# Gates of two units in turns, decays by matrix products, other engines for the fills, and stage dates of a list schedule shifted

## The chip, the cores and the metric

The kernel runs on one core of one Trainium2 chip. A core has five engines that run side by side, each through its own list of instructions in order: TensorE (PE, matrix products), VectorE (DVE), ScalarE (ACT), GpSimd (POOL) and SyncE (SP). SP's part here is to issue DMAs; ACT and POOL issue some too. The metric is the time on the device in microseconds (us); less is better.

## What is computed

Two blocks in a row. The first is a gated linear recurrence for 4 batches, 8 heads, 768 steps and heads of 48 numbers, with complex decays whose magnitude is capped at 0.999. The second is a feed-forward block on its output, seen as 3072 tokens of 384 numbers, with a hidden size of 1536.

```python
mag = np.sqrt(a_re * a_re + a_im * a_im)
scale = np.minimum(mag, 0.999) / (mag + 1e-06)
a_re_n, a_im_n = (a_re * scale, a_im * scale)
for t in range(S):
    new_re = ar * S_re - ai * S_im
    new_im = ar * S_im + ai * S_re
    S_re, S_im = (new_re + outer(k[t], v[t]), new_im)
    y[:, :, t] = q[t] @ S_re
# x: y as (3072, 384)
xn = x / sqrt(mean(x * x) + 1e-06) * rms_g
g = xn @ w_gate
out = (g * sigmoid(g) * (xn @ w_val)) @ w_out
```

The three weight matrices arrive as 64-bit floats and are narrowed to 32 bits on the chip.

## The kernel before

**Chunks, units, groups.** The steps are cut into 24 chunks of 128 (six a batch). Units of chunks go through the gates: unit 0 is chunk 0, unit 1 is chunk 1, and from there each unit has two chunks. Groups of two chunks go through the feed-forward block.

**`gates(u)`** turns a unit's decays into running magnitudes and angles, and rotates q and k by them, so that the recurrence within a chunk becomes ordinary masked attention. Its stages by name: "size" (squares, inverse square roots, and scans that multiply up the squared magnitudes, t4), "root" (inverse square root of t4, one correction step), "turn" (arctangent, scans that add up the angles, reduction to one period, sines), "rot" (products into the tiles `rot`). ScalarE computes inverse square roots, arctangents and sines with tables that have to be loaded: roots and arctangents lie in different ones, and a sine can use the table that the arctangent left. At the end of `gates` the rotated tiles are moved by six DMAs a chunk into `kq` (96 partitions), whose transfers are kept in `moved[n]`, and six DMAs a unit move the chunk's total decays from `ends` into `decay`.

**`attend(n)`** loads v into `ve` and `vn` (six DMAs), computes masked scores into `am` (scores that the mask doesn't write stay at the zeros with which `am` is filled once), multiplies by v and by the state, updates the state by the chunk's products and decay, normalises ("norm": squares, their sum by a product with ones, a power on POOL, spreading to all partitions) and writes `xT`.

**`feed(g, xT)`** multiplies a group's `xT` by the gate and value weights in six blocks, applies the gate into `hT`, and multiplies by `wo`. Groups 0 and 1 do it plainly; from group 2 on four quadrants are combined so that seven products stand for eight, with scratch (S1, S2, T1) in the upper half of `hT`. Group 1 keeps its hidden values in that upper half (`base` 3072).

**`narrow(i)`** loads one of twelve weight pieces by a POOL DMA (three for the gate and three for the value weights, 1.5 MB each, and six for the out weights, 0.75 MB each), lets ACT convert the low words in place and DVE put the 32-bit number together in three operations. At most two pieces are under way (`AHEAD`). The first waits for unit 0's a_im (`GATE`, `begun`), and piece 3, counted from 0, waits until chunk 0's kq has landed:

```python
    CLEAR = {3: 0}
    GATE = 0
```

**What sets the order.** Nothing is issued as the functions run. Each call adds an operation to the class `Flow`, with an engine, a duration, what it reads and writes, and sometimes a date ("due"). `note` finds what an operation depends on by the bounding boxes of what it touches; two transfers whose boxes overlap are planned one after the landing of the other even where their elements don't meet. `dates` carries due dates back from the users to the makers and adds a shift by stage, which is empty before. `schedule` then plays the engines forward in a model of time and lets each take the ready operation with the earliest date, and `issue` writes the result out as the fixed order of every engine. Waits on the chip follow from the data. Arguments: `after` is a dependency, `behind` only an order of issue, `late` the earliest date. Idle stretches of PE before a set time (`WARM`) are filled with matmuls on `rot` whose results nobody reads; they keep PE's clock up.

**The main program** loads the inputs of units 0 and 1, runs `gates(0)`, then `gates(1)`, then the twelve pieces, and then chunk by chunk: the gates of the next unit, attention, and after every second chunk a feed group. After group 2 it adds checks of the weights ("look").

All operations are recorded by the same line, 667 of the kernel before, so the profile tells them apart by tile: `bank` is PSUM, `t`, `in`, `turns` are tiles of the gates, `kin` the raw q and k, and the weight pieces are staged in `wo` and `hT`.

Of the kernel before, what the change touches and what calls it, by code (L numbers as in the profile page):

```python
# [461 lines left out]
class Flow:  # L462
# [7 lines left out]
    LAND = 2.0  # L470
    LANES = 8
    turn = 0.0
    BEGIN = {"SP": 0.8, "ACT": 0.8, "POOL": 0.8}
    TABLES = {"silu": ("S",), "sin": ("S", "T"), "arctan": ("T",), "rsqrt": ("A",)}

# [28 lines left out]
    def note(self, op, ap, write):  # L504
        b = self.box(ap)
        if b is None:
            return
        name, p0, p1, lo, hi = b
        if name.startswith("bank"):
            p0, p1, lo, hi = 0, P, 0, 2048  # L510
        kept = []
        for x in self.seen.get(name, ()):
            o, w, q0, q1, l, h = x
            over = q0 < p1 and p0 < q1 and l < hi and lo < h
            if over and (write or w) and o != op["i"]:
                op["deps"].add(o)
            if not (write and p0 <= q0 and q1 <= p1 and lo <= l and h <= hi):
                kept.append(x)
        kept.append((op["i"], write, p0, p1, lo, hi))
        self.seen[name] = kept  # L520

    def add(self, eng, calls, dur, reads=(), writes=(), table=None, land=None, due=None, after=(), behind=(), late=None, mode=None):
        op = dict(i=len(self.ops), eng=eng, calls=calls, dur=dur, deps=set(), table=table, land=land,
                  base=due, late=late, mode=mode, stage=self.stage, behind={o["i"] for o in behind})
        self.ops.append(op)
        op["deps"].update(o["i"] for o in after)
        for ap in reads:
            self.note(op, ap, False)
        for ap in writes:
            self.note(op, ap, True)  # L530
        return op
# [23 lines left out]
    def schedule(self):  # L555
# [33 lines left out]
        while True:  # L589
            best = None  # L590
            for eng, ops in waiting.items():
                if ops:
                    t = max(free[eng], min(ready[o["i"]] for o in ops))
                    if eng == "SP" and len(sent) >= self.LANES:
                        if "landed" not in sent[-self.LANES]:
                            continue
                        t = max(t, sent[-self.LANES]["landed"])
                    if best is None or t < best[0]:
                        best = (t, eng)
            busy = [q for q in lanes.values() if q]  # L600
            if busy:
                whole = sum(q[0][1]["packet"] for q in busy)
                q = min(busy, key=lambda q: q[0][0] / q[0][1]["packet"])
                t = now + max(0.0, q[0][0]) * whole / q[0][1]["packet"]
                if best is None or t <= best[0]:
                    flows(t)
                    now = max(now, t)
                    o = q.pop(0)[1]
                    o["landed"] = now + o["slow"] + self.LAND + (1.5 if o["eng"] == "POOL" else 0.0)
                    release(o, o["landed"])  # L610
                    continue
            if best is None:
                break
            t, eng = best
            pick = None
            for o in waiting[eng]:
                if ready[o["i"]] > t + 1e-9:
                    continue
                key = o["due"]
                if o["table"] and table not in self.TABLES[o["table"]]:  # L620
                    key += self.switch
                if eng == "PE" and o["mode"] != mode:
                    key += self.turn
                if pick is None or key < pick[0]:
                    pick = (key, o)
            o = pick[1]
            waiting[eng].remove(o)
            dur = o["dur"]
            if o["table"] and table not in self.TABLES[o["table"]]:
                table = self.TABLES[o["table"]][-1]  # L630
                dur += 1.3
                self.loads = getattr(self, "loads", 0) + 1
            if eng == "PE" and o["mode"] != mode:
                mode = o["mode"]
                dur += 0.06
            if eng == "PE" and self.warm and t < self.warm["until"]:
                since = max([free["PE"]] + [x["end"] + self.SYNC for x in self.warm["after"] if not recent])
                n = int((t - since - 0.3) / 0.43)
                if n > 0:
                    self.fillers.append((order - 0.5, n))  # L640
                    recent.append((since, since + 0.43 * n))
            if eng == "PE":
                busy = sum(min(e, t) - max(b, t - 4.0) for b, e in recent if e > t - 4.0)
                if busy < 2.0:
                    dur += min(dur, 3.0)
                recent.append((t, t + dur))
                del recent[:-12]
            o["start"], o["end"], o["order"] = t, t + dur, order
            order += 1
            free[eng] = t + dur  # L650
            release(o, t + dur, self.next)
            if o["land"] is not None:
                flows(t)
                now = max(now, t)
                if eng != "POOL":
                    sent.append(o)
                lanes.setdefault(eng, []).append([o["load"] + 0.05, o])
            else:
                release(o, t + dur)
# [10 lines left out]
def fast(tc, ctx, qT, kT, v, a_re, a_im, w_gate, w_val, w_out, rms_g, out, H, bad):  # L670
# [194 lines left out]
    for t, x in ((ones, 1.0), (halfpi, PI / 2), (mid, -(RE_MAX + RE_MIN) / 2),  # L865
                 (width, -(RE_MAX - RE_MIN) / 2), (mhalf, -0.5), (zeros, 0.0)):
        fill(t, x)
    LATE = 12.0
    for t in ves + states:
        fill(t[:, :, :, D:], 0.0, late=LATE)  # L870
    add("POOL", [(make_identity, (nc, ident), {})], 0.6, [], [ident], late=LATE)
    fill(causal, 1.0, late=LATE)
    for e in range(2):
        for b in range(4):
            x = causal[b * BLK:(b + 1) * BLK, e]
            add("POOL", [(nc.gpsimd.affine_select, (), dict(out=x, in_=x, pattern=[[1, C]],
                                                            compare_op=ALU.is_ge, fill=0.0,
                                                            base=-BLK * (3 - b if e else b),
                                                            channel_multiplier=-1))], 0.3, [x], [x], late=LATE)
    for t in ams:  # L880
        fill(t, 0.0, late=LATE)
    for t in banks[4:6]:
        fill(t, 0.0, eng="DVE")
    dma(gcol, rms_g.rearrange("(c p) -> p c", p=P))


# [15 lines left out]
    AHEAD = 2  # L902
    landed = {}

    CLEAR = {3: 0}

    def fetch(i, piece, raw, eng):
        to, ap, c, f = piece
# [60 lines left out]
    moved = {}  # L969
    HOLD = 1  # L970
    begun = []
    started = []
    cleared = {}
    loaded = {}
# [6 lines left out]
    def load_gates(u):  # L981
# [14 lines left out]
        t["kq"], t["k"], t["q"] = x, x[:, :, 0], x[:, :, 1]  # L996
        for name, ap in (("re", a_re), ("im", a_im)):
            x = dma(t[name], ap[b].rearrange("(h j l) s -> l h j s", j=ND, l=L)[:, :, :, c * C:c * C + T],
                    "ACT" if u < 2 and name == "im" else "SP", behind=moved[HOLD] if u > 1 else ())
            if u < 2 and x["eng"] == "SP":  # L1000
                rows_.append(x)
        if u == GATE:
# [3 lines left out]
    def load_kq(u, t):  # L1006
        flow.stage = "kq", u
        for name, ap in (("q", qT), ("k", kT)):
            for i, n in enumerate(UNITS[u]):
                dma(t[name][:, :, i * C:(i + 1) * C],  # L1010
                    ap[n].rearrange("d (h t) -> (d h) t", t=C).rearrange("(j p) t -> p j t", p=P),
                    behind=moved[HOLD] if u > 1 else rows_)
        return t

    def gates(u):
        ns = UNITS[u]
# [43 lines left out]
        stt(t2, t1, 1.5, t2, ALU.add)  # L1060
        tt(q, q, t4)

        flow.stage = "turn", u
        act(im, im, AF.Arctan, after=[root])
        last = turn.get(u - 1) if ns[0] % NCH else None
        for j in range(ND):
            scan(t3[:, j], im[:, j], zeros[:, 0:T], last[:, j] if last is not None else 0.0,
# [21 lines left out]
        for n_ in ns:  # L1089
            moved[n_] = [dma(kqs[n_ % 2][r:D2:2 * ND], rots[n_ % 2][:, r], "SP") for r in range(2 * ND)]  # L1090
            if n_ < 2:
                cleared[n_] = copy(seen, kqs[n_ % 2][:, 0, 0:1], eng="POOL")
        for r in range(2 * ND):
            dma(decays[way_of(u)][r:D2:2 * ND], ends[:, r % ND, ns[0]:ns[0] + nt], behind=moved[ns[0]])

# [7 lines left out]
    def attend(n):  # L1105
# [1 line left out]
        ve, am, kq = ves[n % 3], ams[n % 2], kqs[n % 2]  # L1107
        first, last = n % NCH == 0, n % NCH == NCH - 1
        vv = vns[0]
        later = dict(behind=moved[min(n - 1, HOLD)] if n else ())  # L1110
        rows = v[n * C:(n + 1) * C, :].rearrange("t (m e d) -> t m e d", e=2, d=D)
        dma(ve[:, :, 0, 0:D], rows[:, :, 0], **later)
        for b in range(4):
# [118 lines left out]
    def feed(g, xT):  # L1232
        flow.stage = "feed", g
        ns = GROUPS[g]
        T = len(ns) * C
        base = {1: 3072}.get(g, 0)
        h = hT[:, base:base + NF * T].rearrange("p (i f t) -> p i f t", i=2, f=NF)
        A = {(i, k): h[:, i, k * HD:(k + 1) * HD] for i in range(2) for k in range(2)}
        S3, S4 = A[1, 0], S2
# [65 lines left out]
        loaded[u] = load_gates(u)  # L1305
    for u in range(2):
        load_kq(u, loaded[u])
    gates(0)
    gates(1)
    for i in range(len(pieces)):  # L1310
        narrow(i)
    gated = 2
    for n in range(N):
        while gated < NU and UNITS[gated][0] <= n:
            gates(gated)
            gated += 1
        xT = attend(n)
        if n == GROUPS[group_of[n]][-1]:
# [13 lines left out]
    for in_, limit, op in ((ef, P_MIN, ALU.is_ge), (ef, 1.0, ALU.is_le), (range_, 0.0, ALU.is_le),  # L1332
# [14 lines left out]
    filler = rots[0][:, 0]  # L1347
    flow.warm = dict(after=started, until=WARM, call=[
        (nc.tensor.matmul, (banks[3][:, 0:C],), dict(lhsT=filler[:, 0:C], rhs=filler[:, C:2 * C], start=True, stop=True))])
    flow.schedule()  # L1350
    with tc.manual_schedule():
        flow.issue()
# [50 lines left out]
```

## Time and profile before

| what | us |
|---|---|
| time, median of three runs | 730.87 (729.05 to 731.51) |
| time of the profiled execution | 727.01 |
| its span, first to last instruction | 725.3 |
| PE busy | 682.6 (94%) |
| DVE busy | 470.0 (65%) |
| ACT busy | 332.3 (46%), 86.0 of it 67 table loads |
| POOL busy | 70.4 (10%) |
| first matmul with a gate weight | 57.33 |

The page divides the span into 40 slices of 18 us and gives each engine a digit of tenths for each; PEclk is PE's granted clock in tenths of full speed. The chain of waits follows the work that ended last back to what released it, with start and length of each piece. A name such as "kq<-rot" reads: written tile from read tile. SPq is SP's queue of DMA issues, and the time given for a DMA instruction there is its issue and not its transfer.

### The profile page before, as it was taken

Reading aid. Unit: us, or ns where it says so; the run is one execution under the profiler, and the core shown is the slowest. Engines: PE = TensorE matmul, PEld = TensorE weight load, DVE = VectorE, ACT = ScalarE, POOL = GpSimd, SP = SyncE. Lnnn points to the kernel's source line nnn. Section 1 sums busy time; section 2 is a strip of 40 time slices with the busy share of each in tenths; the row PEclk is TensorE's granted clock in tenths of the full one; section 3 lists DMA queues with packets and bytes.
Section 4 is the critical chain, followed back from the end, with each engine's and each line's share of the span. In section 5 each row is a group of like instructions: output and inputs, shape, how many; then the busy total and the mean of one; then the engine's idle time right before and its main releaser. Section 6 shows DMA issues by size and latency. Waiting matters only on the chain.

```text
span 725.3 us, 16217 instructions
## 1 busy us (share of the span) xinstructions
PE 682.6 (94%) x6870; PEld 596.2 (82%) x6870; DVE 470.0 (65%) x740; ACT 332.3 (46%) x450; POOL 70.4 (10%) x116
## 2 busy tenths in 40 slices
PE   0579999999999999999999999999999999999996
PEld 0468867886889889889889889889889889889885
DVE  5969898888879878879774656658544333134121
ACT  7639858867385864845461633626310110010010
POOL 6123100001100001011011011011011011000000
PEclk9978999999999999999999999999999999999998
DMA  8696665655466464566533333334133132100000
GB/s 296 214 310 190 194 185 156 180 143 128 132 149 155 142 168 119 164 141 170 140 87 76 85 63 63 100 67 91 42 62 61 37 66 34 36 13 2 23 0 27
DMA packets 105728, 81.84 MB, mean 113 GB/s; under 512 B 43664, under 2 KB 96144, under 8 KB 105648
## 3 DMA queue, kind: packets, MB, share of 16 engines
q1 hardware_dynamic: 100432, 64.99, 32.9%
q0 software_dynamic: 4416, 15.35, 9.2%
q8 instruction: 56, 0.92, 0.5%
q10 hardware_dynamic: 800, 0.39, 0.2%
q14 instruction: 24, 0.20, 0.1%
HBM read 55.84 MB, written 4.72 MB: 83 GB/s over the span
## 4 chain that ended last, share of the span: by engine, by line
PE 83%; DVE 5%; DMA 4%; ACT 3%; SPq 2%; issue 1%; POOL 0%; DVEq 0%; ACTq 0%
PE bank L667 83%; DMA ve<-in_v_dram 2%; SPq L667 2%; ACT turns L667 1%; DVE rot L667 1%; DVE turns L667 1%; DMA wo<-in_w_gate_dram 1%; ACT t L667 1%; ACT L667 1%; DMA kq<-rot 1%; DVE hT L667 1%; DMA in<-in_a_re_dram 1%; DVE in L667 0%; DVE t L667 0%; DVE wo L667 0%
## 5 line engine op out<-in xcount | busy, mean ns | idle before, releaser
L667 PE MATMUL bank<-xT,wg 128*128 128x256 f32 x864 | 200.9, 383 | 0.9 <-DVE xT L667 0.9
L667 PE MATMUL bank<-xT,wv 128*128 128x256 f32 x864 | 201.2, 382 | 0.4 <-DVE xT L667 0.4
L667 PEld LDWEIGHTS bank<-xT,wg 128*128 128x128 f32 x864 | 162.2, 191 | 22.8 <-DVE xT L667 1.1
L667 PEld LDWEIGHTS bank<-xT,wv 128*128 128x128 f32 x864 | 161.3, 190 | 23.5 <-issue 1.6
L667 ACT ACTIVATE sg<-bank 128x512 f32<-128x512 f32 x72 | 43.0, 597 | 169.4 <-PE bank L667 168.8
L667 PE MATMUL bank<-wo,hT 128*128 128x192 f32 (+1 forms) x576 | 117.7, 356 | 0.6 <-DVE hT L667 0.6
L667 DVE TENSOR_TENSOR hT<-bank,sg 128x512 f32<-128x512 f32 x72 | 49.5, 688 | 100.1 <-PE bank L667 88.5
L667 PEld LDWEIGHTS bank<-wo,hT 128*128 128x128 f32 x576 | 95.7, 190 | 12.9 <-DVE hT L667 1.1
L667 ACT ACT_TABLE_LOAD x67 | 86.0, 1283 | 16.1 <-DVE rot L667 7.1
L667 POOL TENSOR_TENSOR rs<-ssv,mhalf 128x1 f32<-128x1 f32 x24 | 25.3, 1054 | 498.6 <-DVE ssv L667 468.2
L667 DVE TENSOR_TENSOR rot<-kin,turns 128x768 f32<-128x768 f32 x48 | 44.1, 952 | 3.8 <-DMA kq<-rot 3.4
L667 PE MATMUL bank<-sums,hT 128*128 128x192 f32 x240 | 44.2, 327 | 0.0
L667 ACT ACTIVATE kt<-bank 128x384 f32<-128x384 f32 x40 | 19.2, 486 | 51.9 <-PE bank L667 32.3
L667 ACT ACTIVATE turns<-in 128x768 f32<-128x768 f32 (+1 forms) x39 | 30.1, 791 | 26.5 <-DVE rot L667 14.2
L667 PE MATMUL bank<-am,ve 128*32 128x128 f32 x768 | 39.2, 281 | 0.9 <-DMA ve<-in_v_dram 0.9
L667 PEld LDWEIGHTS bank<-sums,hT 128*128 128x128 f32 x240 | 39.7, 190 | 0.1
L667 PEld LDWEIGHTS bank<-kq 96*32 96x32 f32 x1536 | 30.2, 110 | 10.9 <-issue 7.0
L667 DVE TENSOR_TENSOR hT<-hT 128x768 f32<-128x768 f32 x40 | 38.2, 956 | 0.6
L667 PE MATMUL bank<-kq 96*32 96x128 f32 (+3 forms) x1536 | 35.2, 235 | 3.0 <-DMA kq<-rot 2.9
L667 PE MATMUL bank<-rot 128*128 128x128 f32 x64 | 12.2, 352 | 24.8 <-DVE rot L667 24.8
L667 DVE COPY_PREDICATED am<-causal,bank 128x512 f32<-128x512 int32 x48 | 33.9, 724 | 1.6 <-PE bank L667 1.1
L667 ACT ACTIVATE t<-t 128x768 f32<-128x768 f32 (+1 forms) x39 | 30.9, 792 | 8.7 <-DVE t L667 8.2
(115 smaller groups left out, 741.9 us busy)
## 6 DMA issues: line engine op xcount, KB each, us to landing
kq<-rot SPq DMA_DIRECT2D x144, 128.0 KB, 3.0
kin<-in_q_dram SPq DMA_DIRECT2D x24, 192.0 KB, 3.3
kin<-in_k_dram SPq DMA_DIRECT2D x24, 192.0 KB, 3.4
wo<-in_w_gate_dram SPq DMA_DIRECT2D x6, 768.0 KB, 5.0
out_dram<-ot SPq DMA_DIRECT2D x24, 192.0 KB, 2.2
wo<-in_w_val_dram SPq DMA_DIRECT2D x6, 768.0 KB, 5.7
wo<-in_w_out_dram SPq DMA_DIRECT2D x6, 768.0 KB, 4.3
in<-in_a_re_dram SPq DMA_DIRECT2D x11, 384.0 KB, 6.1
```

Source lines behind the costliest of these rows:

```text
L667: fn(*args, **kw)
```

## The change

It has six parts.

1. `gates` becomes a generator that stops after "root". Units 0 and 1 are run in turns: both up to the roots, then both from the turns on. The arctangent now depends on the last two units' roots.
2. `send_decays` is new. For units 0 and 1 the decays reach `decay` by a product with a selection matrix `pick` and a copy from PSUM, not by six DMAs each. The matrices for it (`pick`, `band`, `head`) are made once at the start in tiles that are free then. Later units send by DMA as before.
3. The fills: `am` 0 and the pads of `ve` and the states go from POOL to DVE, `am` 1 to a ScalarE copy of zeros, `ident` is made first, and the causal mask is cut by five selections and not eight.
4. `CLEAR` lets weight piece 3 wait for chunk 1's kq and not chunk 0's, and group 1's `hT` base is 0.
5. The planner: operations of one `group` (a chunk's v transfers, a unit's q and k transfers) don't depend on each other; ACT and DVE may be left idle in the plan for up to 1.5 us when a far more urgent operation is about to become ready; the fillers' start is counted only once their source is planned; the first loads get early dates.
6. A table of some 90 shifts of due dates by stage and number.

```diff
@@ Flow.note, Flow.add
-            if over and (write or w) and o != op["i"]:
+            if over and (write or w) and o != op["i"] and (not op["group"] or self.ops[o]["group"] != op["group"]):
                 op["deps"].add(o)
...
@@ Flow.schedule
+            if eng in self.patient:
+                for x in waiting[eng]:
+                    if t < ready[x["i"]] < t + o["dur"] - 0.2 and x["due"] < o["due"] - 50.0 and ready[x["i"]] < t + 1.5:
+                        pick = None
+                        free[eng] = max(free[eng], min(ready[y["i"]] for y in waiting[eng] if t < ready[y["i"]]))
+                        break
+                if pick is None:
+                    continue
...
@@ fast, at the start
+    add("POOL", [(make_identity, (nc, ident), {})], 0.5, [], [ident], due=-150.0)
...
+    fill(ams[0], 0.0, eng="DVE", due=-290.0)
+    act(ams[1], zeros[:, 0:C].unsqueeze(1).to_broadcast([P, H, C]), AF.Copy, due=-290.0)
     for t in ves + states:
-        fill(t[:, :, :, D:], 0.0, late=LATE)
...
-    for t in ams:
-        fill(t, 0.0, late=LATE)
...
+        fill(t[:, :, :, D:], 0.0, eng="DVE", due=-280.0)
+    pick = ots[0][:, 0:ND * D2].rearrange("p (r x) -> p r x", r=ND)
+    band, head = (ots[1][:, o:o + n] for o, n in ((0, P // H), (16, H)))
+    own = [ots[1][:, o:o + ND * H].rearrange("p (r h) -> p r h", r=ND) for o in (32, 64)]
+    fill(pick, 0.0, eng="DVE", late=LATE)
+    for o, order in ((band, "p (x h) -> p x h"), (head, "p (x h) -> p h x")):
+        add("DVE", [(nc.vector.tensor_reduce, (), dict(out=o, in_=ident.rearrange(order, h=H), axis=mybir.AxisListType.X,
+                                                       op=ALU.add))], 0.3, [ident], [o], late=LATE)
+    for r in range(ND):
+        o = pick[:, r].rearrange("p (x j) -> p x j", j=2 * ND)[:, :, r::ND]
+        copy(o, band.unsqueeze(2).to_broadcast([P, P // H, 2]), late=LATE)
...
-    CLEAR = {3: 0}
+    CLEAR = {3: 1}
...
+    def send_decays(u):
+        ns = UNITS[u]
+        if u < 2:
+            tt(own[u], ends[:, :, u:u + 1].to_broadcast([P, ND, H]), head.unsqueeze(1).to_broadcast([P, ND, H]))
+            ps = banks[u][0:D2, 0:H]
+            mms([(ps, pick[:, r], own[u][:, r], r == 0, r == ND - 1) for r in range(ND)], 0.5)
+            copy(decays[u][:, :, 0], ps)
+            return
+        for r in range(2 * ND):
+            dma(decays[way_of(u)][r:D2:2 * ND], ends[:, r % ND, ns[0]:ns[0] + len(ns)], behind=moved[max(ns[0], 1)])
...
@@ gates
+        roots.append(root)
+        yield
         flow.stage = "turn", u
-        act(im, im, AF.Arctan, after=[root])
+        act(im, im, AF.Arctan, after=roots[-2:])
...
@@ feed
-        base = {1: 3072}.get(g, 0)
+        base = 0
...
@@ main program
-    gates(0)
-    gates(1)
+    firsts = [gates(0), gates(1)]
+    for x in firsts * 2:
+        next(x, None)
...
-            gates(gated)
+            list(gates(gated))
...
+    flow.shift = {
+        ("attend", 1): 2.2, ("attend", 2): -6.5, ("attend", 4): -25.0, ("attend", 6): -11.5, ("attend", 8): 2.6,
...
+        ("w", 0): -2.4, ("w", 1): 1.0, ("w", 2): 0.3, ("w", 5): -13.7, ("w", 6): 5.7, ("w", 8): -5.6,
+        ("w", 10): 7.1, ("w", 11): 6.2,
+    }
```

## The prediction

> **What bounds the kernel now.** I read the page from the top, then the chain of waits in order of time, then the issues of SP's queue, then the busy time by stage. The page first:
>
> ```profile
> span 725.3 us, 16217 instructions
> ...
> PE   0579999999999999999999999999999999999996
> ...
> PEclk9978999999999999999999999999999999999998
> ```
>
> TensorE (PE) is full from the fourth slice on; only the first 60 us have room, and there the granted clock falls too. So a gain has to come from the start, and the view to ask is what the first feed group (its first matmul is at 57.33) waited for. The chain of waits, in order of time (start, length, what):
>
> ```profile
> 24.79 0.55 SPq L667
> ...
> 30.54 8.23 DMA ve<-in_v_dram
> 38.78 0.59 SPq L667
> ...
> 40.28 6.54 DMA ve<-in_v_dram
> ...
> 46.96 4.48 PE bank L667 x64
> ...
> 53.79 1.21 POOL rs L667
> ...
> 55.04 26.66 PE bank L667 x118
> ```
>
> The attention of chunk 1 (matmuls at 46.96) waited for its v rows (ve), which went out late and landed slowly. SP's issues say why they were late:
>
> ```profile
> 22.46 4.16 SPq L667 DMA_DIRECT2D kq<-rot  x6
> 26.66 3.84 SPq L667 DMA_DIRECT2D decay<-ends  x6
> 30.54 0.60 SPq L667 DMA_DIRECT2D ve<-in_v_dram  x1
> 33.67 3.79 SPq L667 DMA_DIRECT2D kq<-rot  x6
> 37.73 3.16 SPq L667 DMA_DIRECT2D ve<-in_v_dram  x4
> ```
>
> Chunk 0's q and k, six decays, one v transfer, then a wait until unit 1's rotated q and k are ready (33.67), then the rest of v. Last, the busy time by stage (columns: PE, PE's weight loads, VectorE (DVE), ScalarE (ACT), POOL, clock, DMA share, GB/s):
>
> ```profile
> 0.00:57.33 57.33, 25.30 (x368) 22.50 (x369) 44.05 (x62) 35.34 (x58) 20.08 (x46) 0.90 0.85 266
> 57.33:101.20 43.87, 43.16 (x393) 35.95 (x392) 41.33 (x56) 34.51 (x44) 6.29 (x12) 0.98 0.68 206
> ```
>
> Of the 25.30 us of PE before 57.33, 12.2 are fillers (bank<-rot, x64). After 57.33 PE runs to 718.84 with about 4.2 us of idle (by windows: 0.7 to 101.2, 0.7 to 119.5, 0.7 to 140, 0.55 around 231, 0.3 in 280 to 360, 0.9 around 672, 0.4 in the tail). DVE is busy 41.33 of 43.87 us in the second stage: it is the next limit, just behind PE.
>
> **What the Trainium skill says.** "ScalarE: Activation LUTs", What ACT_TABLE_LOAD costs: 1283 ns, plus a drain of some 1380 ns. Here a load shows as 1.28 us (13.56) and the next ACTIVATE follows 0.01 us behind it (14.85), so I use 1.28. "DMA: Bandwidth & Descriptors", Queues, rings and completion order: each DMA engine takes turns between its queues packet by packet. The trace agrees with contention: ve lands in 2.4 us in the median, but in 8.23 and 6.54 us while 1.5 MB weight pieces move. "TensorE: Matmul & The Clock Gate", What's actually happening: a PE idle for a window of some 3.4 us falls to half clock. Here the clock is 0.54, 0.50 and 0.59 in the three 5 us stretches from 45 on, after 1.88 us busy in 40 to 45. "VectorE: DVE Perf Modes", Zero memsets can be issued as uint32 (trn2): a memset takes one cycle per element; here 128x512 takes 485 ns, 0.95 ns each.
>
> **The change, part by part.** Own time of the profiled execution: 727.01 us (span 725.3, 1.7 around it); the median shown is 730.87, a factor 1.0053. The sum is made against the former.
>
> *Gates in turns.* Units 0 and 1 pass their square roots both before either arctangent, so two of the four table loads up to 18.12 (at 13.56 and 18.12) go: 2.57 us of ACT. Unit 0 pays a little: unit 1's scans end at 11.91, its root takes 0.51, the load 1.28, so unit 0's arctangent starts near 13.7 instead of 13.02. From there by the durations of before: arctangent 0.52, scans 1.1, integer copy 0.51, reduction 0.56, absolute value and two sines 1.62, product 0.95, rotation 0.96: end at 20.0, if nothing of a weight piece lies between; with one block of it (1.76 at most) 21.7. I take 21, before 22.43. Unit 1 follows with one product and one rotation more (1.9), and I let piece 0's narrowing (0.95 + 1.76 + 1.75 = 4.5) lie between for half: 25, where before it ended at 34.5.
>
> *Decays by products.* Twelve DMA issues leave SP: 3.84 us before ve of chunk 1, the other six after it (at 47.73 and 55.08). kq of unit 0 then goes out in 21 to 25, kq of unit 1 in 25 to 29, ve of chunk 1 (5 x 0.6 = 3.0) by 32. Landing 2.4 without and 6.5 to 8.2 us with a weight piece in the way. CLEAR now lets the fourth piece go only when unit 1's kq has landed (about 32), so ve meets one piece at most: I take 5 us, landed at 37 against 46.82. New work: on DVE a fill of 288 elements, two reductions of 128, five small copies and two small products. Such reductions take 0.94 us for 768, small DVE operations about 0.15, so 0.3 + 0.35 + 0.75 + 0.3 = 1.7; on PE six matmuls of 8 columns, under 1.8 us by the 0.30 us of the 128x1 matmuls. PE waits then anyway. The DVE part counts in the DVE sum below. The new wait, PE for ends and DVE for PE, holds up the next DVE operation by some 0.5 us twice at worst; I take none and keep 1 us for the range.
>
> *Fills.* One am (1024 elements, 0.97) and the pads of ves and states (5 x about 0.27) go to DVE, the other am to ACT (about 1.0 by 0.52 for 384, less the start). DVE has done its bank fills at 2.03 and starts on data at 5.92: 2.03 + 2.3 = 4.35, hidden with 1.5 to spare; ACT ends its warm-up at 3.02 and starts at 4.81, so 1.0 fits with 0.8 to spare. POOL has less to do, but its first weight fetch (4.54) waits for a_im to land (4.42): gain 0. If a fill comes late it costs its overrun, 0.5 at most.
>
> *Loads in groups.* Only the dates: v and kq transfers are no longer planned one after the landing of the other. What it moves is counted above. *Patient engines, shifted dates, base 0 of group 1's hT*: no operation is added or removed; the order changes. Bounds: of the 4.2 us idle after 57.33 all could go (-4.2), or the moved dates cost as much (+4); the hT area of group 1 no longer lies where later scratch (T1, S1, S2) is written. I take -1.
>
> *From ve to the first feed.* Before 46.96 to 57.33, 10.4 us at half clock. At full clock the attention of a chunk takes 2.0 (chunk 2, from 97.86) instead of 3.6, and the small sums 0.8 for 1.4; so 8.4 if the fillers reach that far: 37 + 8.4 = 45.4. The first weight block then takes 2.75, not 3.63. PE's start is 11.9 + 0.9 = 12.8 us earlier.
>
> *What is late next.* DVE must have narrowed all twelve weight pieces, which it does at 101.2, having been busy 44.05 + 41.33 = 85.4 us. It can't start on data before 5.92; without any idle, with 1.7 us of new work and 0.97 of fills before, it would end at 5.92 + 84.4 + 1.7 = 92.0: 9.2 earlier and no more. PE from 45.4 has gates and values for 32 us (57.33 to 90.30 less 0.9), to 77.4, then products with the first w_out pieces for 5.3, to 82.7; the next products need pieces 8 and 9, narrowed at 93.1 before and 84 to 85.5 now, and attention 2 needs kq that came at 95.5 before. So PE runs dry for 2 to 4 us; I take 3.5. Sum: 12.8 - 3.5 + 1 = 10.3. Own time 727.0 - 10.3 = 716.7; times 1.0053 = 720.5, and I take 720.
>
> **The rivals.**
> *A, DVE or the weights take half of it:* PE starts early, but DVE keeps 5 of its 10.9 us of idle after 5.92 (handoffs to ACT don't vanish), so the last piece comes 4 to 5 us earlier: -4.5, 726.4. For: 41.33 of 43.87. Against: PE can do attention and early products meanwhile.
> *B, all is kept:* no dry spell, and 2 us of the idle go: -15, 715.8. For: 18.3 us up to 119.5 hold 11.7 us of DVE work for unit 3 and weight checks that can wait. Against: the sum of 92.0 above.
> *C, slower:* the fourth piece (fetch at 29.38, landed 38.4) now waits for unit 1's kq. If narrowing keeps DVE and kq still lands at 41.5, the piece lands near 50.5; the sixth, which waits for it, goes out at 50.5 and not 43.57; w_out hangs behind its narrowing: +5, 735.8. It decides once kq 1 lands later than about 35 (29.4 and 6 us between landing and narrowing of the sixth piece). Against: 2.57 us of ACT and 3.84 us of SP are gone before it.
> *D, no change:* the orders trade off, 731.
>
> **How the numbers follow.** Forecast 0.50 (7 to 14 us: 717 to 724 after the factor), A 0.20, B 0.13, C 0.12, D 0.05. Range 711 to 728.5: the forecast with the unknown costs (+4, +1, +0.5), A whole, and B down to 711; C and D lie outside. Faster by over 0.3% (about what a measurement of this kernel can tell from no change) 0.83, within it 0.05, slower 0.12.
>
> **What would show it.** Right: two table loads before 18 us, not four; no decay issue on SP before 40; the second six kq issues at 24 to 29; the fourth piece's fetch near 32; first matmul with wg at 43 to 47 with the clock at 1.00 before it; a gap of some us in PE between 77 and 90; DVE above 95% busy from 6 to 92. Wrong: kq 1 landing after 35, the half clock again before the first feed, or new PE idle beyond 120, where the order now frozen would differ from what the chip does.

## The result, and the profile after

Measured: 725.54 us median of 20 runs (720.3 to 732.0) against 728.77 us (725.43 to 732.29, 20 runs) for the kernel before in the same series. The ratio is 0.9961, 95% interval [0.994, 0.9981], so 2.8 us faster (0.0039 of 728.8). The ratio leaves out one slow run of the changed kernel, the one at 732.0. The forecast was 10 us, from a base that was itself 2.1 us too high: the median of three runs, 730.87, stands against 728.77 here. The profiled execution took 725.97 us with a span of 724.2; before it was 727.01 and 725.3. The page after:

```profile
span 724.2 us, 16265 instructions
...
PE   0769999999999999999999999999999999999996
...
PEclk9977999999999999999999999999999999999998
```

TensorE (PE) is full from the same slice on as before, and the clock still falls in slices 3 and 4. So the start that the forecast wanted 12 us earlier did not come forward. The chain of waits after, in order of time (dots for shorter pieces left out), says what held it:

```profile
30.14 1.67 DVE wg L676
31.81 1.27 DVE am L676 x2
...
34.28 2.35 DMA kq<-rot
...
36.79 1.96 issue
...
38.82 0.74 issue
...
40.15 0.74 POOL wo L676
40.89 6.66 issue
...
47.58 3.62 POOL junk L676
51.20 0.72 POOL hT L676
51.92 3.02 issue
...
54.99 2.01 POOL rs L676
...
57.04 0.81 PE bank L676 x2
...
58.55 4.43 PE bank L676 x12
```

The v rows (ve), on which the chain hung before, are gone from it. In their place stands chunk 1's kq, which landed near 36.7 (before about 41.6), and then 22 us of small steps in queues that work in order. SP's issues after:

```profile
23.43 3.80 SPq L676 DMA_DIRECT2D kq<-rot  x6
27.28 2.58 SPq L676 DMA_DIRECT2D ve<-in_v_dram  x4
29.96 4.92 SPq L676 DMA_DIRECT2D kq<-rot  x6
```

No decays, as forecast, and kq of chunk 1 goes out 3.7 us earlier than before (33.67). Now the time by stage. I cut it where PE begins group 1's gates: by then every kernel here has done the same work (72 matmuls with wg and 72 with wv of group 0, its 48 products with wo, attention of chunks 0 to 3). Columns: PE, its weight loads, VectorE (DVE), ScalarE (ACT), POOL, clock, DMA share, GB/s. After:

```profile
0.00:58.55 58.55, 28.83 (x399) 26.45 (x399) 46.77 (x79) 39.45 (x64) 19.37 (x35) 0.88 0.84 271
58.55:122.70 64.15, 61.62 (x624) 48.79 (x624) 58.24 (x82) 40.02 (x56) 11.13 (x15) 0.98 0.59 163
122.70:717.60 594.90, 593.92 (x5884) 526.38 (x5878) 370.43 (x595) 248.30 (x330) 36.50 (x56) 1.00 0.37 93
```

The same stages of the kernel before (its first is known from the prediction):

```profile
57.33:119.56 62.23, 60.81 (x625) 48.16 (x624) 57.53 (x83) 46.29 (x63) 8.05 (x14) 0.99 0.65 188
119.56:718.85 599.29, 596.45 (x5884) 525.56 (x5878) 367.91 (x595) 250.62 (x331) 42.24 (x56) 1.00 0.37 91
```

In these two executions PE reaches the cut 3.1 us **later** than before (122.70 for 119.56), and needs 4.4 us **less** from there (594.9 for 599.3; 1.9 of it is idle time, 2.84 less 0.98, and the rest shorter busy time for the same matmuls). The gain lies where I had put 1 us, and the early part, where I had put 9.3, gave a loss. How large the loss is stays uncertain: the two stages add up to 1.3 us and not to the 2.8 measured, since the execution of before ran 1.8 us under its median and that of after 0.4 over. The time after the cut is nearly the same in all kernels of this order (last section), so 2.8 us in all would leave a loss of some 1.6 before it, an estimate.

Why the start stood still, by engine. POOL's queue after:

```profile
36.77 2.04 POOL L676 COPY seen<-kq 96x1 f32<-96x1 f32 x1 [4.92 <-DMA kq<-rot]
38.75 0.78 POOL L676 DMA_DIRECT2D wo<-in_w_val_dram  x1
39.56 0.59 POOL L676 TENSOR_TENSOR rs<-ssv,mhalf 128x1 f32<-128x1 f32 x1
...
47.58 3.62 POOL L676 COPY junk<-wo 1x1 int32<-1x1 int32 x1 [6.68 <-DMA wo<-in_w_val_dram]
...
54.99 2.00 POOL L676 TENSOR_TENSOR rs<-ssv,mhalf 128x1 f32<-128x1 f32 x1 [3.06 <-DVE ssv L676]
```

The first line is the copy that waits for chunk 1's kq (`CLEAR`), and behind it stand the fourth piece's fetch and chunk 0's power (rs), whose input was ready at 36.23. VectorE waited for that power, by way of the spreading product on PE, and then had weight steps ahead of the masks of chunk 1:

```profile
41.11 0.55 DVE L676 TENSOR_TENSOR xT<-yg,bank 128x384 f32<-128x384 f32 x1 [2.34 <-PE bank L676]
41.58 1.75 DVE L676 SCALAR_TENSOR_TENSOR wg<-hT,wg 128x1536 int32<-128x1536 int32 x1
43.37 1.76 DVE L676 CUSTOM_DVE_ANT_0 wg<-hT,wg 128x3072 uint16<-128x3072 uint16 x1
45.04 1.33 DVE L676 COPY_PREDICATED am<-causal,bank 128x512 f32<-128x512 int32 x2
```

ScalarE converts the fourth piece, which came late, ahead of chunk 1's squares (sq):

```profile
51.23 1.60 ACT L676 ACTIVATE wo<-wo 128x1536 int32<-128x1536 uint32 x1 [3.14 <-POOL junk L676]
52.69 0.52 ACT L676 ACTIVATE sq<-bank 128x384 f32<-128x384 f32 x1
```

The masks of the kernel before:

```profile
43.87 1.33 DVE L667 COPY_PREDICATED am<-causal,bank 128x512 f32<-128x512 int32 x2
```

So the masks are 1.2 us later than before, though kq came 4.9 us earlier. PE still ended chunk 1's attention earlier, at 48.28 and not 50.59. But the squares that follow came at 52.69, behind the fourth piece, and not at 50.68 as before, and the first gate matmul starts at 58.55, not 57.33.

### The profile page after: what moved, and what is told of

It is laid out like the page before. It is cut to its first block, busy times and chain, and to the rows that moved or that the text cites. A ratio compares the mean times of both kernels' runs of the same rounds, so it can differ in the third digit from the quotient of the medians.

```text
span 724.2 us, 16265 instructions
## 1 busy us (share of the span) xinstructions
PE 684.4 (95%) x6900; PEld 601.6 (83%) x6900; DVE 476.0 (66%) x756; ACT 327.8 (45%) x448; POOL 67.0 (9%) x106
## 4 chain that ended last, share of the span: by engine, by line
PE 85%; DVE 5%; issue 3%; DMA 2%; ACT 2%; POOL 1%; SPq 1%; POOLq 0%; DVEq 0%; ACTq 0%
PE bank L676 85%; DMA kq<-rot 2%; DVE wo L676 1%; DVE rot L676 1%; SPq L676 1%; DVE turns L676 1%; DMA in<-in_a_re_dram 1%; ACT t L676 1%; DVE wv L676 1%; POOL junk L676 1%; DVE wg L676 0%; DVE hT L676 0%; POOL rs L676 0%; ACT L676 0%; ACT turns L676 0%
## 5 line engine op out<-in xcount | busy, mean ns | idle before, releaser
L676 POOL TENSOR_TENSOR rs<-ssv,mhalf 128x1 f32<-128x1 f32 x24 | 20.6, 858 | 485.1 <-DVE ssv L676 469.6
L676 PE MATMUL bank<-kq 96*32 96x32 f32 (+3 forms) x1536 | 35.3, 236 | 3.7 <-DMA kq<-rot 3.2
L676 PE MATMUL bank<-am,ve 128*32 128x128 f32 x768 | 36.9, 275 | 0.0
L676 PE MATMUL bank<-kq,state 96*32 96x128 f32 x640 | 32.2, 272 | 0.0
```

Of the source, the lines that this page charges most:

```text
L676: fn(*args, **kw)
```

## The experiments

The first eleven, up to e16, keep the planned order of the changed kernel, unless said, and edit it after `flow.schedule()`: `ops(stage, engine, dma)` lists a stage's operations on an engine in their order (with True its DMAs alone, with False the others), and `put(x, y, d)` gives x the place of y plus d. Dots stand for lines left out. Ratios are against the kernel before in the same series; "start" is the first matmul with a gate weight in the profiled execution (58.55 in the changed kernel).

### Is the start what counts?

**e1_norm_first**: ScalarE does chunk 1's norm before it converts the fourth piece.

```diff
+    put(ops(("w", 3), "ACT")[0], ops(("norm", 1), "ACT")[-1], 0.3)
```

> The changed kernel with its order kept but for one thing: ScalarE converts the low words of the fourth weight piece after the squares and scalings of chunk 1's norm, not before. Theory T1 (the start was lost in the queues: chunk 1's norm stood behind a weight piece that had not come): the squares start near 48.5 us, not 52.7, the sum products follow near 49, and the first matmul with the gate weights comes at 55 to 56 instead of 58.55, since POOL's power still stands behind its landing copy and a DMA issue until about 52; time 2 to 3.5 us less than the changed kernel. Theory T2 (VectorE's work up to the last weight piece sets the end, whatever the start does): the first gate matmul is earlier too, but PE's idle after it grows by as much; time within 1 us of the changed kernel.

Measured 0.9937 [0.9918, 0.9956], 723.44 us; start 54.84. **e2_copy_aside**: POOL's landing copies read another word of the piece, so that ScalarE doesn't wait for the copy as well.

```diff
+    for i in range(12):
+        o = ops(("w", i), "POOL", False)[0]
+        n = places[i].shape[1]
+        o["calls"] = [(nc.gpsimd.tensor_copy, (), dict(out=junk, in_=places[i][0:1, n - 1:n]))]
```

> The changed kernel with its order kept; POOL's landing copies read a word that ScalarE doesn't overwrite, so that ScalarE's conversion waits for the transfer alone and no more for POOL's copy. T1, in its form that the copy of 3.6 us at 47.58 was held on POOL by VectorE while the piece had landed: ScalarE starts the fourth piece near 47.6 and not 51.2, the squares near 49.3, the first gate matmul at 55 to 56; time 2 to 3.5 us less. Rival (the piece itself landed only at 51.2 and the copy's length is that wait): nothing moves, 0. T2: the first gate matmul earlier, time within 1 us.

Measured 0.9964 [0.9944, 0.9983], start 56.34. **e3_power_first**: chunk 0's power goes ahead of the copy for `CLEAR` and of the fourth piece's fetch.

```diff
+    put(ops(("rot", 1), "POOL", False)[0], ops(("norm", 0), "POOL", False)[0], 0.1)
+    put(ops(("w", 3), "POOL", True)[0], ops(("norm", 0), "POOL", False)[0], 0.2)
```

> The changed kernel with its order kept but for POOL: chunk 0's power goes ahead of the copy that waits for chunk 1's q and k, and of the fourth piece's DMA behind it. T1: the power runs at 36.3 to 38 and not 39.56, VectorE's product into xT at 38 to 39 and not 41.11, what stands behind it (two weight steps, the masking of chunk 1's scores at 45.04) moves up by 2 to 3 us, and the first gate matmul with it unless the fourth piece holds it; time 0 to 3 us less. T2: time within 1 us.

Measured 0.9973 [0.9946, 1.0], start 57.53. **e4_all_three**: the three edits together.

> The three edits together. T1: first gate matmul at 51 to 53 us instead of 58.55, half clock before it shorter, time 5 to 7 us less than the changed kernel (about 719 against 725.5). T2: first gate matmul as early, but gaps of 4 us or more in PE between it and 125 us that the changed kernel doesn't have; time within 2 us.

Measured 0.9951 [0.9928, 0.9973], start 54.62. **e6_masks_early**: e4, and chunk 1's masks before the weight steps.

```diff
...
+    for i, o in enumerate(ops(("w", 2), "DVE")[1:]):
+        put(o, am1[1], 0.1 + 0.1 * i)
...
+    for i, o in enumerate(late):
+        put(o, ssv1, 0.02 + 0.02 * i)
```

> The three edits of e4 and VectorE's order changed in one place: chunk 1's masking goes ahead of the last two steps of the third weight piece, and its norm's small step ahead of three operations of unit 2. T1: first gate matmul near 50 to 51 us, against 54.6 in e4 and 58.6 in the changed kernel; if what is gained at the start stays, time 3.5 to 4.5 us less than e4. T2 and T3: the first gate matmul is as early as that, but PE's idle between 75 and 125 us grows by about as much; time within 1 us of e4.

Measured 0.9945 [0.9926, 0.9965], start 54.52. The power was spread at 50.56, but the steps moved back now lay ahead of xT; e6's PE:

```profile
50.56 0.74 PE L676 MATMUL bank<-ident,rs 128*128 128x128 f32 x2 [1.66 <-POOL rs L676]
...
54.52 2.08 PE L676 MATMUL bank<-xT,wg 128*128 128x256 f32 x4 [2.79 <-DVE xT L676]
```

**e11_one_table**: e1, and a one-column sine before the first arctangent, so that the table loaded there serves both.

```diff
...
+    first["calls"] = [(nc.scalar.activation, (), dict(out=warm, in_=warm, func=AF.Sin))] + first["calls"]
```

> The first edit (e1), and one sine of a single column ahead of the first arctangent, so that the table loaded there serves the sines too: table loads up to 25 us 2 and not 3 (the one at 19.10 goes), unit 0's and unit 1's rotated q and k 1 us earlier. T1: time 0.5 to 1.2 us less than e1. T2, T3: 0, within 0.5 us.

Measured 0.9943 [0.9921, 0.9965], start 53.54. **e12_warm**: e1, and 16 fillers before the spreading product.

```diff
+    spread = ops(("norm", 1), "PE")[1]
+    spread["calls"] = flow.warm["call"] * 16 + spread["calls"]
```

> The first edit (e1), and 16 more filler matmuls (about 2.5 us) while PE waits for chunk 1's power before the first feed: the clock stays full, the first gate block takes 2.75 and not 4.2 us. If PE's start matters (T1): 1 to 1.5 us less than e1. If what comes later sets the end (T2, T3): within 0.5 us.

Measured 0.9927 [0.9902, 0.9953], start 55.65, the first block at 2.86 us and not 4.18 as in e1. What follows from the seven: the queues did hold the start, and freeing ScalarE's brings it 3.7 us forward (the squares begin at 48.53, not 52.69), but the time follows by some 1.7 us (0.9937 against 0.9961, with overlapping intervals), and 1 us earlier again (e11) or at full clock (e12) adds nothing that can be told from zero. T1 had asked 5 to 7 us of e4 and 3.5 to 4.5 more of e6; their ratios give 0.7 and 0.4. So an earlier start alone isn't shown to bring more than e1's share, and most of it is given back later.

### What takes it back?

The largest waits of PE in e1's profiled execution (total, times, longest) between 57 and 130:

```profile
PE bank L676 <- DMA decay<-ends: 3.3, 1, 3.3
PE bank L676 <- issue: 2.9, 1, 2.9
PE bank L676 <- DVE hT L676: 0.9, 1, 0.9
```

That execution took 729.86 us, the longest of its series, so the sizes aren't typical (in the changed kernel's the wait for chunk 2's kq was 1.4 us). The place of the largest is: chunk 2's inputs, landing while weight pieces move. **e5_hold_last**: e1, and the last two weight pieces wait for chunk 2's kq, with ScalarE's conversion of the first of them moved back too.

```diff
...
+    p10["calls"] = [(nc.gpsimd.tensor_copy, (), dict(out=seen, in_=kqs[0][:, 0, 0:1]))] + p10["calls"]
+    put(p10, kq2, 0.3)
+    put(p11, kq2, 0.4)
...
```

> The first edit (norm ahead of the fourth piece on ScalarE) and one more: the last two out-weight pieces are sent only when chunk 2's rotated q and k have landed, and ScalarE converts the eleventh behind chunk 2's transposed keys. T3 (the earlier start is given back near 95 us, because chunk 2's q and k then share the DMA engines with two weight pieces): chunk 2's last q and k transfers land in 3 to 4 us and not 9, PE's wait near 95 to 98 (3.3 us with the first edit alone) falls to 1 or less, time 2 to 3 us less than with the first edit alone (723.4). T2 (VectorE sets the end): the wait goes but another of the same size comes where the last pieces are needed, time within 1 us of the first edit. Rival within T3: the pieces themselves, now 5 us later, stall the products at 110 to 120 us; then 0 to 2 us more.

Measured 0.995 [0.9928, 0.9973]. The wait at 98 us was gone; two of 0.9 and 1.0 us for ScalarE at 103 and 106 had come. The 2 to 3 us that T3 had asked for did not. **e10_half_out**: e1, and half of each out-weight piece isn't loaded (the rest of its tile keeps what lay there).

```diff
...
+        ops(("w", i), "POOL", True)[0]["calls"] = [(fn, args, dict(out=kw["out"][:, 0:1], in_=kw["in_"][:, 0:1]))]
```

> The first edit (e1), and of each of the six out-weight pieces only one of its two rows is loaded (the other half keeps what lay there): 2.4 MB less for the DMA engines between 60 and 97 us, nothing else changed. T3: chunk 2's q and k land in 3 to 4 us, PE's waits near 95 and 109 us (3.3 and 2.9 us in e1's profile) go; 3 to 5 us less than e1. T2: 0 to 1.5 us less.

Measured 0.9922 [0.9898, 0.9947]; 2.4 MB less and 1 us, inside the intervals, where T3 had asked 3 to 5. **e9_less_dve**: e1, and VectorE skips the second narrowing step of ten pieces (12.8 us of it; the weights are then other numbers).

```diff
+    for i in range(2, 12):
+        shift, both = ops(("w", i), "DVE")[0:2]
+        shift["calls"][0][2].update(scalar2=0x3FFFFFFF, op1=ALU.bitwise_and)
+        both["calls"] = []
```

> The first edit (e1), and VectorE leaves out the second step of narrowing in weight pieces 2 to 11 (the exponents then aren't put together, so the weights are other numbers): 4 x 1.76 + 6 x 0.96 = 12.8 us of VectorE less between 41 and 119 us, with the order kept. T2 (VectorE's work sets the end of the start-up): of the 12.8 us a large part comes back, 5 to 9 us less than e1 (723.4, that is 714 to 718). T3 (transfers set it): 1 to 3 us less.

Measured 0.9879 [0.9853, 0.9904], by the ratios 4.2 us below e1, with intervals that don't touch. That is more than T3 allowed (1 to 3) and less than T2 asked (5 to 9). The stages of its profiled execution, the shortest of its series (715.44 us; the median is 718.8), with the columns of above:

```profile
0.00:51.90 51.90, 26.43 (x398) 25.00 (x398) 43.77 (x77) 36.41 (x61) 13.79 (x35) 0.93 0.83 264
51.90:112.44 60.54, 60.07 (x625) 47.71 (x625) 49.44 (x74) 42.89 (x59) 9.18 (x15) 1.00 0.72 210
112.44:707.06 594.62, 593.87 (x5884) 526.38 (x5878) 370.37 (x595) 248.53 (x330) 36.49 (x56) 1.00 0.37 93
```

The second stage is PE's own work, 60.07 us, and next to nothing else. The start came earlier too, at 51.90 for e1's 54.84. How much of the 4.2 us came by way of POOL, whose small operations VectorE's steps stretch (last section), wasn't separated. **e16_lean** has both edits of e9 and e10:

> Chunk 1's norm ahead of the fourth piece's conversion, with VectorE's second narrowing step of pieces 2 to 11 left out (the weights are then other numbers) and half of each output-weight piece left unloaded (the rest of its tile holds what lay there). If VectorE and the transfers are two separate costs: ratio 0.9879 - 0.0015 = 0.9864 or below. If the lighter VectorE alone was what the early stretch lacked and the transfers are then hidden: 0.987 to 0.989.

Measured 0.9854 [0.9816, 0.9892]. The point estimate adds up, but the interval holds e9's value: that the transfers are a cost beside VectorE's isn't shown. That VectorE's work is a cost, is.

### What carries the measured gain?

**e7_no_shift**: the change with an empty shift table, planned anew. **e13_dates_alone**: the kernel before with the shift table. **e14_early_dates**: the change with only the 29 shifts of the weights and of chunks and units 0 to 2. **e15_late_dates**: the change with only the other 55. **e17_before_late_dates**: the kernel before with those 55. **e18_late_norm_first**: e15 with e1's edit. All six are planned anew and differ only in this table (e18 in e1's edit too), of which e15's first lines stand for the rest:

```diff
     flow.shift = {
-        ("attend", 1): 2.2, ("attend", 2): -6.5, ("attend", 4): -25.0, ("attend", 6): -11.5, ("attend", 8): 2.6,
+        ("attend", 4): -25.0, ("attend", 6): -11.5, ("attend", 8): 2.6, ("attend", 11): 1.7, ("attend", 12): 1.6, ("attend", 13): 0.9,
...
     }
```

> The changed kernel without its table of shifts (all stage dates as computed); the order is planned anew, so many things move. If the shifts carry the gain: 3 us or more over the changed kernel, that is no better than the kernel before (728.5). If they do nothing on the chip: within 1.5 us of the changed kernel.

> The kernel before with nothing but the table of shifts. If the dates are the gain and the rest of the change is nothing (the reading from the run with the empty table): ratio 0.994 to 0.998, PE idle after 120 us near 1 us. If the dates only fit the order that the other parts make: 0.998 to 1.006, and the change's gain is then in the two together.

> The change with only those 29 shifts that belong to chunks and units 0 to 2, feed 0 and the weights. If the gain is made in the first 120 us: ratio 0.994 to 0.998. If it is made in the long even part after 120 us: 0.998 to 1.001, with 2.5 to 3 us of PE idle after 120 us.

> The change with only the other 55 shifts (unit and chunk 3 on, feed 1 on). If the gain is made after 120 us: ratio 0.994 to 0.998 and about 1 us of PE idle there. If in the first 120 us: 0.998 to 1.001.

> The kernel before with only the 55 late shifts. If the late dates alone are the gain: ratio near 0.992, as with the rest of the change. If they need the changed early part (gates in turns, decays by products, fills): 0.998 to 1.002, and then the structure does carry its share, which the early shifts took away again.

> The change with the late shifts only and the fourth piece's conversion behind chunk 1's norm on ScalarE. First gate product from 55.15 to about 53.5. If the early start is worth what it was before (0.0024 for 3.7 us): ratio 0.990 to 0.991. If later waits take it back: 0.9916 or above.

Measured (the three columns of times are from the profiled executions; the cut is the one of above):

| kernel | ratio, 95% interval | last weight piece narrowed | cut | cut to PE's end |
|---|---|---|---|---|
| before | 1 | 101.2 | 119.56 | 599.3 |
| before, all shifts (e13) | 1.001 [0.9993, 1.0027] | 111.8 | 120.26 | 601.2 |
| before, late shifts (e17) | 0.999 [0.9968, 1.0011] | 99.9 | 119.11 | 596.7 |
| change, no shifts (e7) | 0.9995 [0.9981, 1.001] | 100.9 | 121.80 | 599.4 |
| change, early shifts (e14) | 1.0037 [1.0008, 1.0067] | 118.8 | 125.98 | 598.1 |
| change, late shifts (e15) | 0.9916 [0.9884, 0.9948] | 98.5 | 120.97 | 594.1 |
| change, late, norm first (e18) | 0.9921 [0.9895, 0.9946] | 97.7 | 118.56 | 594.1 |
| change, all shifts | 0.9961 [0.994, 0.9981] | 115.6 | 122.70 | 594.9 |

Of the last columns, PE's row for the third stage in e7, and below it in e15 (columns: PE busy, clock, DMA share, GB/s):

```profile
121.80:721.23 599.43, 598.13 (x5878) 1.00 0.37 91
```

```profile
120.97:715.10 594.13, 593.84 (x5878) 1.00 0.37 92
```

Equal matmuls, 4.3 us less busy time and 1.0 us less idle. Part of the 4.3 is the clock, which in e7 fell once more just behind the cut (columns as for the stages above):

```profile
120.00:140.00 20.00, 18.94 (x209) 15.74 (x200) 16.30 (x22) 15.74 (x17) 0.61 (x1) 0.91 0.41 112
```

20 us at 0.91 are a loss of some 1.8 us, an estimate; in the profiles of before, e15, e17 and the changed kernel these 20 us show 1.00 (e13 has 0.91 from 320 to 340). From 130 us on the products of 192 columns with wo took 85.1 us in e7 and 84.3 in e15, the kq scores together 29.6 and 29.0; their order had moved, and what makes up the rest isn't settled. What follows: neither the change without dates nor all the dates on the kernel before give a gain. The 55 late shifts on the changed kernel give 0.8%, where on the kernel before they give 0.1% (the intervals of e15 and e17 don't touch). How far they need the rest of the change the traces leave open: behind the cut they take 2.5 us from the kernel before too (599.3 to 596.7), against 5.3 from the changed one (599.4 to 594.1), of which the 1.8 of e7's clock must be taken off; why e17's time, over 22 runs, shows no more than 0.1% of it (0.3% at most by its interval) isn't known. The early shifts cost about 0.4%: e14 against e7 and all shifts against e15 give the same size, each with intervals that just overlap; with e1's edit in both (e1 against e18) it is 0.2%, not resolved. They put gates of the next units ahead of weights on VectorE: with them the last piece is narrowed at 115.6 and 118.8, without at 100.9 and 98.5. That this is how they cost time is argued, not shown: the cut doesn't follow the last piece (100.9 and 121.80 in e7, 115.6 and 122.70 with all shifts). With late shifts alone the masks of chunk 1 stand ahead of the weight steps again; e15's VectorE:

```profile
39.72 1.76 DVE L676 CUSTOM_DVE_ANT_0 wg<-hT,wg 128x3072 uint16<-128x3072 uint16 x1
41.40 0.15 DVE L676 TENSOR_SCALAR ssv<-bank 128x1 f32<-128x1 f32 x1
41.47 1.32 DVE L676 COPY_PREDICATED am<-causal,bank 128x512 f32<-128x512 int32 x2
...
43.14 0.56 DVE L676 TENSOR_TENSOR xT<-yg,bank 128x384 f32<-128x384 f32 x1
```

e15 and e18 have the lowest ratios with the whole computation (723.13 and 722.28 us), with intervals clear of 1; against the changed kernel they are 0.4% lower, with intervals that just overlap. e18 starts 2.1 us before e15 (53.04 and 55.15) and is no faster, and e13 starts at 52.32, 5.0 us before the kernel before, and is no faster than that: the start isn't the bound. Which part of the change the late shifts need (transfers in groups, patience, the other `hT` base) wasn't tried.

### Does the moved `CLEAR` cost?

**e8_clear_chunk0**: the change with the old clearance, planned anew.

```diff
-    CLEAR = {3: 1}
+    CLEAR = {3: 0}
```

> The changed kernel with the fourth weight piece waiting for chunk 0's q and k as before, and not chunk 1's; planned anew. T1 in its form that the late fourth piece (fetch at 38.75, used at 51.2) is what held the start: fetch near 31, first gate matmul 3 to 6 us earlier, time 2 to 4 us less. Rival: the piece then shares the DMA engines with chunk 1's q and k and v, which land 4 to 6 us later as in the kernel before; time the same or up to 3 us more.

Measured 0.9944 [0.9919, 0.997] against 0.9961 [0.994, 0.9981] with {3: 1}: not resolved. T1's earlier start didn't come. The early fourth piece delays chunk 1's kq, as the rival had it; e8's largest waits of PE from 40 to 126, in an execution 5 us over its median:

```profile
PE bank L676 <- DMA kq<-rot: 7.4, 2, 5.3
PE bank L676 <- POOL rs L676: 2.9, 1, 2.9
```

The start was 60.37 there, 1.8 us later, and the median time no longer.

## Why the prediction was wrong

The sign was right and the time lies in the range, but by luck: every early term of the sum failed, the start did not come forward at all, and the gain came from the dates, where the sum had next to nothing.

**Table loads.** "At 13.56 and 18.12, go": one went. After, loads stand at 1.52, 13.81 and 19.10. Before, unit 1's arctangent at 23.92 had no load because the table of the sines served it too; after, both arctangents came first, with a table that has no sine, and the sines needed the third load. The Trainium skill says in "ScalarE: Activation LUTs", Table sets: the hidden batching unit, that sets and not functions have to be batched; e11, where a sine comes first, has one load fewer, which agrees. It gained no time. So "a sine can use the table that the arctangent left" holds only where a sine had loaded it, as at 23.92. The sign "two table loads before 18 us" came true to the letter (1.52 and 13.81), with the third just behind, at 19.10.

**Rotation and kq.** Unit 1's rotation ended at 30.14, not 25, and kq 1 went out at 29.96 to 34.88, not 25 to 29; its landing came 4.9 us earlier, not the 9 the step implied. One reason is my reading of unit 0's end before: 22.43 was the end of the first of its two rotations, the second ended at 24.76. The sum for unit 0 counts one rotation (0.96) and after it shows two (22.45 to 24.28, where I had 21).

**"From ve to the first feed", the step that failed.** I carried ve's landing forward through an unchanged chain: "37 + 8.4 = 45.4". The 37 was about right: kq had landed near 36.7, four of chunk 1's five v transfers had landed by 31.45, the fifth went out at 34.92, and PE waited for none. The start was 58.55, so the 8.4 was some 22. Between the landing and the start lie operations of four engines, each in a fixed queue, and the change put others ahead of them: `CLEAR`'s copy and the fetch on POOL, two weight steps on VectorE, the fourth piece's conversion on ScalarE. e1 shows that the last alone cost the start 3.7 us. The half clock stayed too (first block 4.42, not 2.75). The profile of before had a warning: the chain names the v rows because they came last, but PE's wait for them was 0.9 us, and the masks that the same products need came only at 43.87 to 45.20.

```profile
L667 PE MATMUL bank<-am,ve 128*32 128x128 f32 x768 | 39.2, 281 | 0.9 <-DMA ve<-in_v_dram 0.9
```

And an earlier start would not have carried to the end: of e1's 3.7 us some 1.7 were left, where the sum kept 9.3 of 12.8.

**"What is late next".** The sum "92.0" for the last narrowed piece assumed that a VectorE with less idle time spends what it gains on weights. From 6 to 92 us it was busy 75.13 us after and 75.12 before, 87%, not the 95% foreseen, and the early shifts gave this time to gates: the last piece came at 115.6. So the term wasn't "9.2 earlier and no more" but 14 later, and the part before the cut lost 3.1 us in the profiled pair. That VectorE's work limits this part was right, and e9 shows it, but only for a third: 12.8 us less of its work brought 4.2 us.

**"I take -1" for the dates.** The bounds were ±4 and I took the middle's near side because no operation is added; it was the term that decided. The cut-to-end stage gave -4.4, and e15 against e7 shows that the late shifts make it on the changed kernel; how far they need the rest of the change is open. The early ones of the same table seem to cost about 3 us (0.4%), which no term of mine had.

**Right.** No decay issue on SP before 40; the fills hid in the first 5.5 us; the decays' products cost no step on the chain of waits. **Rival A** (VectorE or the weights take half) named the mechanism nearest to e9, and its 726.4 is near the 725.54 measured, but by chance: PE did not start early, and the last piece came 14 us later, not 4 to 5 earlier. **Rival C**'s late fourth piece happened: fetched at 38.75, landed near 47.5. Its price came through ScalarE's queue; that an undisturbed kq (e8) paid it back is likely but not resolved.

## What to carry to other kernels

Before an earlier arrival is carried to the end of a chain, list for each engine on the way what the new fixed order puts ahead of the next link, and ask what comes second behind the wait that the chain names; a landing moved by 5 us can leave in the queues all that it brought. A table of dates is a change of its own: test it by halves and against an empty table, since one half can hide what the other gains, and since dates may fit only the program they were made for. And compare stages at a cut where the same work is done, not at equal times: here that turned a difference of 1.3 us between two executions into "3.1 lost, 4.4 won".

## What the runs showed of the hardware

- POOL's tiny operations stretch while VectorE works on SBUF (POOL's spans are rough in these profiles): the 128x1 power took 0.59 us at 39.56, with VectorE idle, and 2.00 at 54.99, the 1x1 copy 0.17 at 56.95, with VectorE idle, and 3.62 at 47.58, over four VectorE operations. In e4 the power took 2.90 us at 36.80, over a VectorE operation with one SBUF input and one with two. The Trainium skill says in "GPSIMD Engine Reference", 1. Specifications, that POOL shares its SBUF interfaces with VectorE and contends with its instructions that have two SBUF inputs; these runs agree, and show factors of 5 and 21 between the shortest and the longest.
- In the profiles of the fifteen kernels that have the change and its late shifts, the cut came between 112.4 and 127.6 us (e1 to e4 alone: 120.8 to 127.6), and the rest took 594.1 to 595.3 us each time. The executions of e1 and e4 were 6.4 and 6.5 us over their medians, and all of that lies before the cut (126.6 and 127.6). In them PE stood longer and its clock fell again: 0.87 and 0.81 from 100 to 120 us, where the changed kernel's profile has 1.00. That this is the scatter of every kernel isn't shown, since each was profiled once.
- In some profiles PE stopped inside a group of matmuls with nothing to wait for that the trace shows ("issue", 2.9 us in e1 before 111.93, 3.85 in e4 before 111.59, 0.46 in the changed kernel before 109.70). The cause stays open.
